# One attention-and-MLP kernel: the last attention unit's matrix work in another order

## The chip, the core and the metric

The kernel runs on one core of one Trainium2 chip. The metric is the device time of one execution in microseconds (us); the number given for a kernel is the median of several runs. A profiled execution is a separate run, recorded by the hardware profiler, with a span (first to last instruction) of its own.

## What is computed

A transformer block on 2048 rows of width 576: a layer norm whose scale and shift come from a condition vector, attention over the last 512 cached keys with 32 query heads and 16 key/value heads of width 128, a gated residual, a second such layer norm, a ReGLU MLP of width 4608, and a second gated residual. All of it is float32. Cut to what matters:

```python
h = _layernorm(x) * (1 + ca) + sa
q = (h @ wq)                                  # 32 heads of 128
scores = einsum("bhqd,bhkd->bhqk", q, k) * (Dh ** -0.5)
p = softmax(scores)                           # 512 keys
x = x + ga * (einsum("bhqk,bhkd->bhqd", p, v) @ wo)
h = _layernorm(x) * (1 + cb) + sb
x = x + gb * ((relu(h @ W_gate) * (h @ W_up)) @ W_down)
```

## The kernel before

A float32 operand is split into a high part (`hi`, rounded to the format the TensorE multiplies) and a low part (`lo`, the rest), and a product is made of three matmuls: high by high, high by low and low by high.

**Units.** The attention runs as 128 units (`NU = 128`), one for each pair of a query block of 512 rows and a head; units 0 to 127 are worked in a loop, and work of neighbouring units overlaps. For unit u the loop issues: the scores (`s_half`, 12 matmuls, L496 to L498, into two PSUM tiles `s`) with a transposing maximum on VectorE (L501); `max_pre` (L515, L516) and `sum_pre` of the unit before (L522); `spread` (L530, one small matmul `qm` that carries the maxima of this unit and the sums of the unit before across partitions); `max_bc`, which turns the maxima into a row to subtract; `exp_half` twice; `hi_half` and `lo_half`, which split the exponentials p (ScalarE L577, GpSimd L600); and the sums `ks` (VectorE L606, GpSimd L609). The product with the values (`pv`) of unit u-1 runs during unit u, then `o_mul` (VectorE L641), `o_hi` (ScalarE L645) and `o_lo` (GpSimd L649) make the split output of that unit.

**Output pieces.** Two heads together are multiplied with `wo` in pieces of 128 rows (`piece`, 12 matmuls at L660 into the PSUM tile `wo`, of which there is one buffer, `psW`). A piece takes `ohi` and `olo` of an even and an odd unit. Its result goes to `acc` either on VectorE (L671) or, for a seeded piece, as a copy on ScalarE (L669), which is put into the list `pend_act` and issued at the next `flush(pend_act)`.

**The last unit.** Unit 127 is one of those in which the subtraction of the maximum is done on TensorE (`by_pe`): ScalarE casts the row of maxima (`mr`, L569), and four matmuls with the matrix `minus` (L587) add it, negated, to the scores in PSUM; the exponential (L589) then reads PSUM. The tiles `s` of `psS` have two buffers. The MLP's first pair of products takes one of them: `new_banks` allocates the tile `gu` of the pair from the same pool and tag.

**The MLP.** `mlp_slots` is a generator; each `next` issues one of seven products of a block (two halves of 7 matmuls each at L1004, into `gu`), with pieces of other work between the halves. The steps `M0`, `M1`, `M2` issue the first three products; the first three remaining output pieces of units 124 and 125 (`filler`: `wo_1`, `wo_2`, `wo_3`) stand between their halves.

**What sets the order.** TensorE, VectorE, ScalarE and GpSimd run the instructions in the order in which the program issues them. Beside the loop there is a list of steps with times (`step(name, t, fn)`, unit u at time 10u; `e` is 1280); `run(u, k)` issues all steps up to time 10u+k. Steps of one time go in the order in which they were put down. The order of the DMA queue of SyncE is set by the framework. The three lines around which the rest turns are in the loop:

```python
        else:
            piece(at[10 * u + 1])
            pv_part(u - 1, False)
```

Of the kernel before, what the change touches and what calls it, by code (L numbers as in the profile page):

```python
# [34 lines left out]
def kernel(  # L35
# [120 lines left out]
    def gate_row(j):  # L156
        r = cp.tile([P, D], F32, tag="mrow", name=f"mrow{j}")
        mod_row(j, r, 0.0)
        return r
# [103 lines left out]
    pend, pend_act = [], []  # L263
# [3 lines left out]
    def flush(q=None):  # L267
        q = pend if q is None else q
        while q:
            q.pop()()  # L270
# [178 lines left out]
    NU = HKV * NQB * 2  # L449
# [10 lines left out]
    def unit(u):  # L460
        return UNITS[u]
# [3 lines left out]
    def qproj(u, lo, hi):  # L465
        g, qb, h = unit(u)
        if lo == 0:
            assert ready[qb] == "a"
            ps = psM.tile([P, 512], F32, tag="mm", name=f"qps{u}")
            qst[u] = ps, proj_ops(ps, wqs[h], hT[qb], u in (4, 6))  # L470
        for f in qst[u][1][lo:hi]:
            f()
# [12 lines left out]
    def by_pe(u):  # L485
        return u < PE0 or u >= NU - PE1
# [18 lines left out]
    def by_moves(u):  # L505
        return PE0 <= u < MOVES
# [39 lines left out]
    def sum_inv(u):  # L546
        nc.vector.reciprocal(t5[u + 1][:, 1, :], t5[u + 1][:, 1, :] if by_moves(u + 1) else bps[u + 1][:, 64:80])
# [7 lines left out]
    def max_bc(u):  # L555
        r = bps[u][:, 256:272] if by_pe(u) else t5[u][:, 0, :]
        if not by_moves(u):
            nc.vector.tensor_reduce(r, bps[u][:, :64].rearrange("p (a b) -> p b a", a=4), axis=AX.X, op=ALU.max)
            if u:
                sum_inv(u - 1)  # L560
        m = bp.tile([P, 512], F32, tag="bc", name=f"mb{u}")
        if by_pe(u):
            rr = sp.tile([P, 16, 2], F32R, tag="rr", name=f"rr{u}", bufs=1)
            nc.vector.tensor_copy(rr[:, :, 0], r)
            nc.vector.tensor_sub(rr[:, :, 1], r, rr[:, :, 0].bitcast(F32))
            nc.vector.transpose(m.rearrange("p (b s t) -> p b s t", s=2, t=16),
                                rr.bitcast(F32)[:, :, :, None].to_broadcast([P, 16, 2, 16]))
            bc[u] = bp.tile([P, 512], F32R, tag="bc", name=f"mr{u}")
            nc.scalar.copy(bc[u], m)  # L569
        else:  # L570
            nc.vector.transpose(m.rearrange("p (b j) -> p b j", j=32),
                                r[:, :, None].to_broadcast([P, 16, 32]))
            bc[u] = m
# [24 lines left out]
    def lo_half(u, h):  # L598
        lo_[u, h] = pp.tile([P, 2, 512], F32R, tag="lo", name=f"lo{u}_{h}", bufs=2)
        nc.gpsimd.tensor_sub(lo_[u, h], pt[u, h], hi_[u, h].bitcast(F32))  # L600
# [7 lines left out]
            for j in range(2):  # L608
                nc.gpsimd.tensor_tensor(ks_[u], ks_[u], p[:, j, :], op=ALU.add)  # L609

    def pv_part(u, lows):
        g, qb, hd = unit(u)
        if not lows:
            pvps[u] = psM.tile([P, 512], F32, tag="mm", name=f"pv{u}")
        ps, v = pvps[u], vs[g]
        for kt in range(4):
            a, b = (x[u, kt // 2][:, kt % 2, :] for x in (hi_, lo_))
            if lows:
                nc.tensor.matmul(ps, v[:, kt, :], b, start=False, stop=kt == 3)
            else:  # L620
                nc.tensor.matmul(ps, v[:, kt, :], a, start=kt == 0, stop=False)
                nc.tensor.matmul(ps, v[:, 4 + kt, :], a, start=False, stop=False)
        if lows:
            done[u] = pvps.pop(u)
# [18 lines left out]
    def o_hi(u):  # L643
        ohi[u] = op.tile([P, 512], F32R, tag="ohi", name=f"ohi{u}")
        nc.scalar.copy(ohi[u], o[u])  # L645

    def o_lo(u):
        olo[u] = op.tile([P, 512], F32R, tag="olo", name=f"olo{u}")
        nc.gpsimd.tensor_sub(olo[u], o.pop(u), ohi[u].bitcast(F32))  # L649
# [33 lines left out]
    w_use, pieces, seeds = set(), [], {}  # L683
# [590 lines left out]
    def step(name, t, fn, *args):  # L1274
        sched.append((t + PLAN.get(name, 0), len(sched), fn, args))

    HOOK = (0, 4, 6, 9)
    e = 10 * NU
# [11 lines left out]
    def setd(d, k, fn):  # L1290
        def go():
            d[k] = fn()
        return go
# [144 lines left out]
    step("m5.l", 1046, m5_back)  # L1438
    step("gb", 1059, setd(mods, "gb", lambda: gate_row(5)))

    step("T.ohi2", e, o_hi, NU - 2)
    step("T.olo2", e, o_lo, NU - 2)
    lay0, lay = lay_steps()
# [104 lines left out]
    mlp = mlp_slots()  # L1548
# [54 lines left out]
    mat(0, 1, lambda: h_back(0, "B22"))  # L1603
    for n, t in enumerate((1245, 1265, 1275)):
        step("w0", t, w_prep, n)
    step("M0", e, next, mlp)
    step("M1", e + 1, next, mlp)
    step("T.pv0", e + 2, pv_half, NU - 1, 0)
    step("T.pv1", e + 2, pv_half, NU - 1, 1)
# [10 lines left out]
    def run(u, k):  # L1620
        t = 10 * u + k
        while sched and sched[-1][0] <= t:
            fn, args = sched.pop()[2:]
            fn(*args)

    for u in range(NU):
        u0, q0 = (u - 4, 3) if u % 2 else (u - 3, 1)
        u1, q1 = (u - 2, 0) if u % 2 else (u - 3, 2)
        if u0 > 0:
            pieces.append((10 * u + (3 if u + 1 < NU else 1), u0, q0))  # L1630
        if u1 > 0:
            pieces.append((10 * u + 6, u1, q1))
    at = {t: n for n, (t, _, _) in enumerate(pieces)}

    run(-1, 9)
    for u in range(NU):
        run(u, 0)
        if u > 1 and u % 2 == 0:
            o_hi(u - 2)
            o_lo(u - 2)  # L1640
        s_half(u, 0)
        s_half(u, 1)
        run(u, .5)
        max_pre(u)
        if u:
            sum_pre(u - 1)
        if by_moves(u):
            cross(u)
            max_bc(u)
        run(u, 1)  # L1650
        if u + 1 < NU:
            qproj(u + 1, 0, 14)
        else:
            piece(at[10 * u + 1])
            pv_part(u - 1, False)
        run(u, 2)
        if not by_moves(u):
            spread(u)
            max_bc(u)
        if u + 1 < NU:  # L1660
            q_hi(u + 1)
        run(u, 3)
        if 10 * u + 3 in at:
            piece(at[10 * u + 3])
        if u > 1 and u % 2:
            o_hi(u - 2)
            o_lo(u - 2)
        run(u, 4)
        if u + 1 == NU:
            pv_part(u - 1, True)  # L1670
        elif u:
            pv_half(u - 1, 0)
        flush(pend_act)
        exp_half(u, 0)
        flush()
        run(u, 5)
        exp_half(u, 1)
        if late_hi(u):
            hi_half(u, 0)
        if u:  # L1680
            if by_moves(u):
                sum_inv(u - 1)
            sum_bc(u - 1)
        if u + 1 < NU:
            q_lo(u + 1)
        ksum_op(u, 0)
        ksum_op(u, 1)
        run(u, 6)
        if 0 < u < NU - 1:
            pv_half(u - 1, 1)  # L1690
        if 10 * u + 6 in at:
            piece(at[10 * u + 6])
        run(u, 7)
        if u:
            o_mul(u - 1)
        flush()
        run(u, 8)
        hi_half(u, 1)
        flush(pend_act)
        lo_half(u, 0)  # L1700
        lo_half(u, 1)
        run(u, 9)
# [56 lines left out]
```

## Time and profile before

| | |
|---|---|
| median of 3 runs | 2860.71 us (2859.68 to 2861.39) |
| the profiled execution's own time | 2863.24 us |
| its span | 2861.5 us |
| mean granted TensorE clock in it | 0.997 |
| attention units, about | 45 to 1606 us of the span |
| the stretch that the change reorders | 1583 to 1614 us |
| MLP, about | 1592 to 2861 us |

In the profile PE is TensorE's matmuls, PEld its weight loads, DVE is VectorE, ACT ScalarE, POOL GpSimd, SPq the DMA queue of SyncE. A timeline row gives the start in us from the span's start, the busy time, the engine, line and operation, output and inputs by name, and the count; in brackets stands the idle time before it and what ended it. A matmul's busy time is pipelined (0.39 us for one of 512 columns, of which the next starts 0.23 us later), so that stalls are read best from the starts of the weight loads, one to each matmul.

### The profile page before, as it was taken

How to read it: one execution, taken by the hardware profiler on the slowest of the kernel's cores; microseconds unless marked ns; L12 is line 12 of the kernel's file. 1: busy time of each engine (PE TensorE's matmuls, PEld its weight loads, DVE VectorE, ACT ScalarE, POOL GpSimd, SP SyncE). 2: the span in 40 equal slices, each digit the busy share in tenths (PEclk: the TensorE clock that was granted, in tenths of full speed). 3: DMA queues.
4: the chain of work that ended last, by engine and by line, in shares of the span. 5: the costliest groups of instructions: out<-in, count | busy, mean ns of one | idle time of the engine just before them, and what ended most of it. 6: DMA issues, size and time to landing. Idle time of an engine off the chain costs nothing.

```text
span 2861.5 us, 41171 instructions
## 1 busy us (share of the span) xinstructions
PE 2815.0 (98%) x15006; PEld 2449.6 (86%) x15006; DVE 2247.7 (79%) x3383; ACT 1476.5 (52%) x2105; POOL 2123.3 (74%) x1564
## 2 busy tenths in 40 slices
PE   6999999999999999999999999999999999999999
PEld 5788888888888888888888888888888888888888
DVE  7899999999888998888889756666676466666666
ACT  5666666666766666666656444444444122222221
POOL 5688888888899989877778666777777356655653
PEclk9999999999999999999999999999999999999999
DMA  4012132223233223312244456666667854444443
GB/s 162 24 45 79 65 106 85 83 81 101 96 104 94 92 63 128 106 69 86 72 150 139 157 209 219 233 237 230 234 234 262 337 165 154 153 155 162 155 154 106
DMA packets 164362, 399.57 MB, mean 140 GB/s; under 512 B 15040, under 2 KB 61888, under 8 KB 164160
## 3 DMA queue, kind: packets, MB, share of 16 engines
q1 hardware_dynamic: 132912, 284.84, 30.5%
q10 hardware_dynamic: 31248, 112.11, 9.9%
q8 instruction: 118, 1.93, 0.3%
q14 instruction: 84, 0.69, 0.1%
HBM read 271.16 MB, written 154.57 MB: 149 GB/s over the span
## 4 chain that ended last, share of the span: by engine, by line
PE 82%; POOL 6%; DVE 6%; ACT 2%; issue 2%; DMA 2%; SPq 0%; ACTq 0%; POOLq 0%; DVEq 0%
PE gu L1004 26%; PE wo L660 11%; PE qps L424 11%; PE md L660 8%; PE st_P L1106 6%; PE s L498 3%; PE s L496 3%; PE s L497 3%; PE pv L635 3%; PE pv L634 3%; PE pv L633 3%; POOL lo L600 2%; ACT p L593 1%; DVE t L501 1%; POOL wop L783 1%
## 5 line engine op out<-in xcount | busy, mean ns | idle before, releaser
L600 POOL TENSOR_TENSOR lo<-p,hi 128x1024 fp32r<-128x1024 f32 x256 | 610.4, 2405 | 1.1 <-ACT hi L577 1.1
L609 POOL TENSOR_TENSOR ks<-ks,p 128x512 f32<-128x512 f32 x256 | 351.4, 1373 | 240.3 <-DVE ks L606 133.3
L501 DVE TRANSPOSE_TENSOR_REDUCE t<-s 128x32 f32<-128x1024 f32 x256 | 313.8, 1239 | 85.1 <-PE s L498 75.7
L1004 PE MATMUL gu<-hop_B,wop 128*128 128x512 f32 x1512 | 374.9, 391 | 0.3 <-POOL wop L783 0.2
L1004 PEld LDWEIGHTS gu<-hop_B,wop 128*128 128x128 f32 x1512 | 275.1, 188 | 51.1 <-POOL wop L783 0.9
L1004 PE MATMUL gu<-hop_T,wop 128*128 128x512 f32 x1260 | 316.1, 391 | 0.0
L424 PE MATMUL qps<-hTa,wA 128*128 128x512 f32 x1288 | 309.8, 390 | 5.8 <-DVE hTa L372 2.3
L660 PE MATMUL wo<-woga,ohi 128*128 128x288 f32 x1472 | 298.7, 295 | 1.7 <-POOL woga L183 1.5
L591 DVE TENSOR_TENSOR p<-s,mb 128x1024 f32<-128x1024 f32 x246 | 290.3, 1219 | 4.2
L424 PEld LDWEIGHTS qps<-hTa,wA 128*128 128x128 f32 x1288 | 241.2, 188 | 59.2 <-DVE hTa L372 4.6
L476 ACT ACTIVATE qhi<-qps 128x512 fp32r<-128x512 f32 x128 | 76.4, 597 | 367.2 <-PE qps L424 359.3
L660 PE MATMUL md<-wogb,hhi 128*128 128x288 f32 x1280 | 260.1, 296 | 3.5 <-DVE acc L671 2.6
L660 PEld LDWEIGHTS wo<-woga,ohi 128*128 128x128 f32 x1472 | 246.1, 188 | 18.1 <-POOL woga L183 3.4
L1004 PEld LDWEIGHTS gu<-hop_T,wop 128*128 128x128 f32 x1260 | 227.8, 188 | 38.9
L577 ACT CAST hi<-p 128x1024 fp32r<-128x1024 f32 x256 | 259.5, 1042 | 1.5
L593 ACT ACTIVATE p<-p 128x1024 f32<-128x1024 f32 x246 | 249.5, 1052 | 13.8 <-DVE p L591 13.4
L671 DVE TENSOR_TENSOR acc<-md,acc 128x576 f32<-128x576 f32 x160 | 120.8, 755 | 165.0 <-PE md L660 164.6
L660 PEld LDWEIGHTS md<-wogb,hhi 128*128 128x128 f32 x1280 | 213.1, 189 | 16.5 <-DVE acc L671 4.2
L1115 DVE TENSOR_TENSOR acc<-st_P,acc 128x576 f32<-128x576 f32 x160 | 121.0, 756 | 127.9 <-PE st_P L1106 127.9
L660 PE MATMUL wo<-woga,olo 128*128 128x288 f32 x736 | 217.8, 296 | 1.3 <-POOL olo L649 1.2
L660 PE MATMUL md<-wogb,hlo 128*128 128x288 f32 x640 | 189.2, 296 | 0.0
L649 POOL TENSOR_TENSOR olo<-rb,ohi 128x512 fp32r<-128x512 f32 x128 | 167.2, 1307 | 15.3 <-ACT ohi L645 15.1
(278 smaller groups left out, 7094.4 us busy)
## 6 DMA issues: line engine op xcount, KB each, us to landing
wop<-wk_P SPq DMA_DIRECT2D x133, 640.0 KB
wk_P<-wop ACTq DMA_DIRECT2D x119, 640.0 KB
wr<-wlay SPq DMA_DIRECT2D x68, 384.0 KB
rogb<-wd SPq DMA_DIRECT2D x68, 288.0 KB
againq<-akq SPq DMA_DIRECT2D x18, 640.0 KB
rwA<-wq SPq DMA_DIRECT2D x32, 320.0 KB
wlay<-wg SPq DMA_DIRECT2D x36, 256.0 KB
roga<-wo SPq DMA_DIRECT2D x32, 288.0 KB
```

The lines of the kernel that those rows point to most:

```text
L424: return [lambda i=i, a=a, b=b: nc.tensor.matmul(ps, a, b, start=(i == 0), stop=(i == n - 1)) for i, (a, b) in enumerate(ops)]
L501: nc.vector.tensor_reduce(t5[u][:, 2 * h:2 * h + 2, :].rearrange("p k b -> p (k b)"), t.rearrange("p k (b j) -> p (k b) j", j=32), axis=AX ...
L577: nc.scalar.copy(hi_[u, h], pt[u, h])
L591: nc.vector.tensor_tensor(p, t, bc[u][:, None, :].to_broadcast([P, 2, 512]), op=ALU.subtract)
L593: nc.scalar.activation(p, p, AF.Exp, bias=0.0, scale=1.0)
L600: nc.gpsimd.tensor_sub(lo_[u, h], pt[u, h], hi_[u, h].bitcast(F32))
L609: nc.gpsimd.tensor_tensor(ks_[u], ks_[u], p[:, j, :], op=ALU.add)
L649: nc.gpsimd.tensor_sub(olo[u], o.pop(u), ohi[u].bitcast(F32))
L660: nc.tensor.matmul(ps[:, half, :H2], a[:, sl], w[b][:, cs], start=(n == 0 and seed is None), stop=(n == 5), skip_group_check=seed is not None)
L1004: nc.tensor.matmul(ps, a, c, start=s not in heir(m) and i == 0 and s not in seeds_of(m), stop=i == len(ops) - 1, skip_group_check=True)
L1106: nc.tensor.matmul(ps[:, j, :H2], x[:, sl], w[:, y, :], start=n == 0 and not second, stop=n == 2, skip_group_check=True)
L1115: nc.vector.tensor_tensor(t, ps[:, :, :H2], t, op=ALU.add)
```

## The change

For unit 127 alone, and for the products of unit 126 that fall into it:

- the product of unit 126 with the values is cut: its high parts for the first two key tiles (4 matmuls, L621 and L622) come first, then the small matmul `qm` of unit 127, then the high parts for the other two key tiles (4 matmuls);
- the output piece `wo_0` of units 124 and 125 (12 matmuls) moves from behind the subtraction (L587) to in front of it;
- the low parts of unit 126 (4 matmuls, L619), its `o_mul`, `o_hi` and `o_lo` move behind the MLP's first product, `M0`;
- `M0` comes one step earlier, so that it stands ahead of those low parts;
- `o_hi` and `o_lo` of unit 125 move from unit 127 to the end of unit 126, in front of the two `lo_half` of unit 126;
- `flush(pend_act)` is called right after the first four matmuls of the product, so that the copy of the seeded piece `wo_3` to `acc` (ScalarE L669) comes in front of the cast of the maxima.

No instruction is added or removed.

```diff
-    def pv_part(u, lows):
+    def pv_part(u, lows, kts=range(4)):
         g, qb, hd = unit(u)
-        if not lows:
+        if not lows and not kts[0]:
             pvps[u] = psM.tile([P, 512], F32, tag="mm", name=f"pv{u}")
         ps, v = pvps[u], vs[g]
-        for kt in range(4):
+        for kt in kts:
...
+    step("T.low", e, pv_part, NU - 2, True)
+    step("T.mul", e, o_mul, NU - 2)
     step("T.ohi2", e, o_hi, NU - 2)
     step("T.olo2", e, o_lo, NU - 2)
...
-    step("M0", e, next, mlp)
+    step("M0", e - 1, next, mlp)
...
-            pieces.append((10 * u + 6, u1, q1))
+            pieces.append((10 * u + (6 if u + 1 < NU else 3), u1, q1))
...
             piece(at[10 * u + 1])
-            pv_part(u - 1, False)
+            pv_part(u - 1, False, range(2))
+            flush(pend_act)
         run(u, 2)
...
+        if u + 1 == NU:
+            pv_part(u - 1, False, range(2, 4))
...
-        if u > 1 and u % 2:
+        if u > 1 and u % 2 and u + 1 < NU:
             o_hi(u - 2)
             o_lo(u - 2)
         run(u, 4)
-        if u + 1 == NU:
-            pv_part(u - 1, True)
-        elif u:
+        if 0 < u < NU - 1:
             pv_half(u - 1, 0)
...
-        if u:
+        if 0 < u < NU - 1:
             o_mul(u - 1)
...
         flush(pend_act)
+        if u + 2 == NU:
+            o_hi(u - 1)
+            o_lo(u - 1)
         lo_half(u, 0)
         lo_half(u, 1)
```

TensorE in unit 127, before, from the last high parts of unit 126 (`pv`) through `qm`, the low parts and the subtraction (`s<-mr,minus`) to the piece `wo_0` (the `againo` are weights):

```order
L621 MATMUL pv_16631<-hi_1_16589,againv_16210 128x512
L622 MATMUL pv_16631<-hi_1_16589,againv_16210 128x512
L530 MATMUL qm_16615<-t_127_16605,quad 128x80
L619 MATMUL pv_16631<-lo_0_16594,againv_16210 128x512 x2
L619 MATMUL pv_16631<-lo_1_16596,againv_16210 128x512 x2
L587 MATMUL s_0_16598<-mr_16648,minus 128x512 x2
L587 MATMUL s_1_16607<-mr_16648,minus 128x512 x2
L660 MATMUL wo_0_16677<-againo_16174,ohi_16471 128x288 x2
```

With the change, TensorE at the same place, from the high parts of the second key tile on:

```order
L622 MATMUL pv_16635<-hi_0_16543,againv_16210 128x512
L530 MATMUL qm_16619<-t_127_16609,quad 128x80
L621 MATMUL pv_16635<-hi_1_16589,againv_16210 128x512
L622 MATMUL pv_16635<-hi_1_16589,againv_16210 128x512
L621 MATMUL pv_16635<-hi_1_16589,againv_16210 128x512
L622 MATMUL pv_16635<-hi_1_16589,againv_16210 128x512
L660 MATMUL wo_0_16655<-againo_16174,ohi_16471 128x288 x2
```

and, after the rest of `wo_0`, the subtraction with what follows it, the MLP's first product:

```order
L660 MATMUL wo_0_16655<-againo_16176,olo_16596 128x288
L587 MATMUL s_0_16602<-mr_16649,minus 128x512 x2
L587 MATMUL s_1_16611<-mr_16649,minus 128x512 x2
L1004 MATMUL gu_16693<-hop_B_0_16355,wop_16291 128x512 x2
L1004 MATMUL gu_16693<-hop_B_3_16358,wop_16291 128x512
```

So `qm` has moved in front of four of the high parts, `wo_0` in front of the subtraction, and the first product now follows the subtraction at once; the four low parts come later, between `wo_2` and the second product.

ScalarE in the same stretch, before (`mr` is the cast of the maxima, `p` the exponential, `q` the copy of the first product):

```order
L693 COPY wo_3_16592<-acc_132 128x2x288
L569 CAST mr_16648<-mb_16643 128x512
L645 CAST ohi_16650<-rb_16550 128x512
L669 COPY acc_132<-wo_3_16592 128x576
L589 ACTIVATE p_0_16659<-s_0_16598 128x1024
```

and with the change:

```order
L693 COPY wo_3_16592<-acc_132 128x2x288
L645 CAST ohi_16594<-rb_16550 128x512
L669 COPY acc_132<-wo_3_16592 128x576
L569 CAST mr_16649<-mb_16644 128x512
L589 ACTIVATE p_0_16668<-s_0_16602 128x1024
```

The output cast of unit 125 and the copy of `wo_3` have moved from behind the cast of the maxima to in front of it. Farther down the queue the cast of unit 126's output has moved from in front of the copy `q` to behind it.

On GpSimd the low part of unit 125's output (L649) has moved in front of the two low parts of unit 126's exponentials (L600). On VectorE the addition of `wo_0` to `acc` (L671) moves from behind the sum `ks` (L606) and `o_mul` of unit 126 to in front of the transposes of `rb` (L552), and `o_mul` of unit 126 goes behind the additions of `wo_1` and `wo_2`. On SyncE's queue one load of an MLP weight (`wop`, the sixth) moves in front of two loads `wr`.

## The prediction

> **What bounds the kernel now.** I read the page first.
>
> ```profile
> span 2861.5 us, 41171 instructions
> ...
> PE 2815.0 (98%) x15006; PEld 2449.6 (86%) x15006; DVE 2247.7 (79%) x3383; ACT 1476.5 (52%) x2105; POOL 2123.3 (74%) x1564
> ...
> PE 82%; POOL 6%; DVE 6%; ACT 2%; issue 2%; DMA 2%; SPq 0%; ACTq 0%; POOLq 0%; DVEq 0%
> ```
>
> TensorE is busy 98% of the span and carries 82% of the chain that ended last, so only time in which it stands can be won. The change touches some thirty of 2861 us; what it can win is what TensorE loses there. That is read from the chain of waits in order of time, around unit 127:
>
> ```profile
> 1584.50 4.01 POOL lo L600 x2
> 1588.56 0.74 PE pv L619 x2
> ...
> 1590.33 1.91 PE wo L660 x12
> 1592.24 1.61 PE gu L1004 x7
> ...
> 1597.04 1.58 PE wo L660 x12
> ```
>
> The chain leaves TensorE once: the low parts of unit 126 wait for GpSimd. A clean group of 7 matmuls of 512 columns takes 1.61 us (0.23 each), a clean output piece 1.58; the piece behind the subtraction took 1.91. How long TensorE stood is seen in the timeline, from the starts of the weight loads:
>
> ```profile
> 1585.39 0.19 PEld L621 LDWEIGHTS pv<-hi,againv 128*128 128x128 f32 x1
> ...
> 1586.31 0.42 PEld L530 LDWEIGHTS qm<-t,quad 128*128 128x128 f32 x2
> ...
> 1588.55 0.30 PEld L619 LDWEIGHTS pv<-lo,againv 128*128 128x128 f32 x2 [1.59 <-POOL lo L600]
> ...
> 1589.14 0.76 PEld L587 LDWEIGHTS s<-mr,minus 128*128 128x128 f32 x4 [0.29 <-ACT mr L569]
> ...
> 1590.20 0.30 PEld L660 LDWEIGHTS wo<-againo,ohi 128*128 128x128 f32 x2 [0.30 <-ACT acc L669]
> ...
> 1591.94 1.48 PEld L1004 LDWEIGHTS gu<-hop_B,wop 128*128 128x128 f32 x7
> ...
> 1598.33 0.32 PEld L1004 LDWEIGHTS gu<-hy_T,wop 128*128 128x128 f32 x2
> ```
>
> The orders part at 1585.39, ahead of the last four high parts, and meet at the second product, 1598.33: 12.94 us. Work in it: 12 matmuls of 512 columns (4 high, 4 low, 4 of the subtraction) at 0.23, 2.76; `qm`, 0.22 to the next load (below); three pieces, 4.74; two products, 3.22. Sum 10.94. So TensorE loses 2.00 us here, 0.07% of the time: the most that this stretch can give.
>
> **The change part by part.** No instruction comes or goes, so each term is a wait.
>
> *`qm` in front of four high parts.* It needs the sums of unit 126, which VectorE finishes last. The same step of unit 126, where TensorE had nothing else, shows the delays.
>
> ```profile
> 1573.37 0.70 DVE L522 TRANSPOSE_TENSOR_REDUCE t<-ks 128x16 f32<-128x512 f32 x1
> ...
> 1574.13 0.30 PEld L530 LDWEIGHTS qm<-t,quad 128*128 128x128 f32 x2 [0.30 <-DVE t L522]
> ...
> 1574.35 0.30 PEld L660 LDWEIGHTS wo<-againo,ohi 128*128 128x128 f32 x2
> ...
> 1574.62 0.22 DVE L558 TENSOR_REDUCE t<-qm 128x16 f32<-128x64 f32 x1 [0.54 <-PE qm L530]
> ...
> 1585.44 0.71 DVE L522 TRANSPOSE_TENSOR_REDUCE t<-ks 128x16 f32<-128x512 f32 x1
> ...
> 1586.92 0.23 DVE L558 TENSOR_REDUCE qm<-qm 128x16 f32<-128x64 f32 x1 [0.78 <-PE qm L530]
> ...
> 1588.47 0.62 ACT L569 CAST mr<-mb 128x512 fp32r<-128x512 f32 x1 [5.52 <-DVE mb L566]
> ```
>
> L522 ends at 1586.15 in unit 127, and nothing ahead of it on VectorE moves. `qm` loads 0.06 later (1574.07 to 1574.13), at 1586.21. TensorE reaches it at 1585.39: it now stands 0.82 us where it stood not at all, since the four high parts were the cover. What is won is the maxima: L558 follows the load by 0.49 (1574.13 to 1574.62), so it starts at 1586.70 instead of 1586.92, and the cast `mr`, 1.55 behind it as before, at 1588.25. It ends at 1588.87, and the subtraction can load 0.05 later (1589.09 to 1589.14 before), at 1588.92.
>
> *`wo_0` in front of the subtraction.* From 1586.21 TensorE needs 0.22 for `qm`, 0.92 for four high parts and 1.58 for `wo_0`: 1588.93. So it comes to the subtraction as `mr` is done, and the waits for the low parts (1.59 on the loads), for `mr` (0.29) and for the copy of `wo_3` (0.30) are gone. `wo_0` needs the copy out of the only `psW` buffer and unit 125's split output:
>
> ```profile
> 1582.31 0.64 ACT L693 COPY wo<-acc 128x576 f32<-128x576 f32 x1
> ...
> 1583.78 4.72 POOL L600 TENSOR_TENSOR lo<-p,hi 128x1024 fp32r<-128x1024 f32 x2
> ...
> 1589.69 1.29 POOL L649 TENSOR_TENSOR olo<-rb,ohi 128x512 fp32r<-128x512 f32 x1 [1.19 <-ACT ohi L645]
> ```
>
> ScalarE is free from 1582.95; the cast `ohi`, even if it waits until `wo_3` has used the buffer it takes (near 1584.4), is done by 1585.0, the copy L669, as large as L693's 0.64, follows `wo_3`'s end (just before the high parts, near 1584.9), by 1585.7; `olo` then runs on GpSimd from about 1585.1 to 1586.4. `wo_0` starts at 1587.35. The two `lo` come behind it and end at about 1591.1 instead of 1588.50, with SyncE's next load `wr` behind them; their matmuls now stand at 1597, and that load's first reader (L811, whose first row is at 1621.9) is far off. All this I cost at nothing.
>
> *The first product right behind the subtraction.* It takes a PSUM buffer of the tiles `s`, and these have two: the first half's, free once its exponential has read it. Before, `wo_0` and 1.74 us lay between; now nothing does. The first units show the same reuse, and what it costs:
>
> ```profile
> 47.87 1.02 ACT L589 ACTIVATE p<-s 128x1024 f32<-128x1024 f32 x1 [0.82 <-PE s L587]
> ...
> 48.95 0.29 PEld L496 LDWEIGHTS s<-qhi,kv 128*128 128x128 f32 x1 [1.04 <-ACT p L589]
> ...
> 70.45 0.80 PEld L587 LDWEIGHTS s<-mr,minus 128*128 128x128 f32 x4
> ...
> 71.25 1.03 ACT L589 ACTIVATE p<-s 128x1024 f32<-128x1024 f32 x1 [0.36 <-PE s L587]
> ...
> 1590.05 1.03 ACT L589 ACTIVATE p<-s 128x1024 f32<-128x1024 f32 x1
> ...
> 1592.06 1.02 ACT L589 ACTIVATE p<-s 128x1024 f32<-128x1024 f32 x1
> ```
>
> The exponential starts 0.80 behind the subtraction's first load, takes 1.02, and the next load comes 0.06 after it: 1588.93 + 1.88 = 1590.81. TensorE is through with the subtraction at 1589.85, so it stands 0.96 us. The cover was `wo_0`, which has gone elsewhere.
>
> *The low parts behind the first product.* The first product starts at 1590.81, 1.13 earlier than before, but four low parts (0.92) that were then done are still owed. They wait for nothing at 1597. The second product starts at 1598.33 - 1.13 + 0.92 = 1598.12. **Sum: 0.21 us earlier**; stalls of 0.82 + 0.96 = 1.78 in place of 2.00.
>
> *What is late next.* Behind `M0`, unit 126's `o_mul` waits for the low parts (1598.2 instead of 1591.72), its cast on ScalarE ends near 1599.7, and the casts `hy_T` queued behind it start there.
>
> ```profile
> 1598.05 1.14 ACT L881 CAST hy_T<-lfb 128x512 fp32r<-128x512 f32 x2
> ...
> 1602.22 5.50 POOL L894 TENSOR_TENSOR hz_T<-lfb,hy_T 128x512 fp32r<-128x512 f32 x4
> ...
> 1612.36 0.41 PEld L1004 LDWEIGHTS gu<-hy_T,wop 128*128 128x128 f32 x2
> ...
> 1613.23 1.29 POOL L649 TENSOR_TENSOR olo<-rb,ohi 128x512 fp32r<-128x512 f32 x1 [0.37 <-ACT ohi L645]
> ...
> 1614.69 0.19 PEld L660 LDWEIGHTS wo<-againo,olo 128*128 128x128 f32 x1
> ```
>
> They are 1.6 late, but GpSimd reads them only from 1602.22, and TensorE wants the result at 1612.36. Tight is only the last unit's `olo`: done at 1614.52, loaded at 1614.69. Its chain starts at TensorE's own products and moves with them. I cost both at nothing.
>
> Bounds: if both new stalls were absent, a gain of 2.00; if the product had to wait for the second exponential (1592.06 in place of 1590.05 for the first, so 2.0 more), a loss of 1.8. The value taken lies between, by the rows of units 0 to 2, which show these very waits.
>
> The profiled execution took 2863.24 us, of which 2861.5 are span, and is 2.5 above the median shown; 0.21 less makes 2863.0 there, and 2860.5 for the median.
>
> **Rivals.** *The first product gets the other buffer.* Then it waits for the second exponential: 2.0 later, 0.21 - 2.0 = 1.8 slower than before, 2862.5. It decides if that buffer is the one the pool hands out. For it: nothing in the profile names the buffer. Against: before, the first product loaded at 1591.94, while the second exponential ran from 1592.06. Chance 0.08. TensorE would stand 3 us in one piece, and another row tells what that can cost:
>
> ```profile
> 1914.13 0.85 PE L660 MATMUL md<-wogb,hhi 128*128 128x288 f32 x2 [2.40 <-DVE acc L671]
> ...
> 1914.13 3.23 PE md L660 x12
> ...
> 1900.00:1960.00 60.00, 57.60 (x307) 50.69 (x306) 40.13 (x35) 23.46 (x33) 44.86 (x39) 0.97 0.60 220
> ...
> L811 DVE TENSOR_TENSOR wr<-wr,wr x17: 945/947/6071, 1621.9 to 2195.9; 128x768 f32<-128x768 f32 x17
> ```
>
> After a stall of 2.40 us the next 12 matmuls took 3.23 instead of 1.58 (half speed; the granted clock of that stretch is 0.97): 1.65 more. With that this rival ends at 2864.1. The Trainium skill ("TensorE: Matmul & The Clock Gate", Part 1) has the clock halve after an idle window of about 3.4 us; by it the rival stays at 2862.5. The row at 1914 shows a shorter stall do it, so the measurement decides; the stalls I forecast, 0.82 and 0.96, are under both, and 1.59 here before cost no clock (the product behind it ran in 1.61).
>
> *No stall at the product or at `qm`.* The gain is 2.00, 2858.7. Against: L522's end and the reuse at 48.95. Chance 0.10.
>
> *The MLP falls out differently.* One subtraction of VectorE (L811), right before that stall of 2.40, took 6.07 us instead of 0.95, and the addition behind it (L671) came late; the slow clock added 1.65. A shift of some tenths may undo this, or make another. That is 4.05 either way: 2856.4, or 2864.5. For it: the same operation took between 0.945 and 6.071. Against: nearly all that runs there is released by TensorE and moves with it. Chance 0.11 each. The Trainium skill ("SBUF — State Buffer", "SBUF: two separate sides") says that such an operation and GpSimd hold a shared port pair for a whole instruction; by it the wait would be at most one GpSimd instruction, some 1.3 us by the row of `olo`, and this stall would not be there; the row of 6.07 against 0.95 is longer, so the trace does not agree.
>
> **How the numbers follow.** The forecast, 2860.5, with its own range 2859.7 to 2861.4 (the runs before spread by 1.7), has 0.60; the rivals 0.08, 0.10, 0.11 and 0.11. The range takes in both ends of the MLP's case and all between: 2856.4 to 2864.5. About 0.2% (5.7 us) is what a measurement of this kernel can tell from no change; no case reaches it alone, two together would: faster 0.03, within 0.2% 0.93, slower 0.04.
>
> **What would show it.** In the changed profile: `qm`'s load waits 0.8 us on L522; the subtraction waits for nothing or a tenth; the first `gu` load waits about 1 us on the exponential L589; the low parts wait for nothing; the second product comes 12.7 us after the fifth high part's place instead of 12.9. I am wrong if the first product starts without a wait or only after the second exponential, or if the MLP shows one stall of 2 us more or less.

## The result, and the profile after

| | before | changed |
|---|---|---|
| median, first comparison (22 runs each) | 2861.03 us (2856.68 to 2868.05) | 2865.05 us (2861.85 to 2869.15) |
| mean | 2860.87 | 2865.47 |
| ratio of the times | | 1.0017, 95% interval 1.0011 to 1.0023 |
| profiled execution, span | 2861.5 | 2866.8 |
| granted TensorE clock | 0.997 | 0.997 |

The change makes the kernel 0.17% slower, some 4.6 us by the means. The page of the changed kernel answers to the lines shown of before:

```profile
span 2866.8 us, 41171 instructions
...
PE 2816.5 (98%) x15006; PEld 2450.9 (85%) x15006; DVE 2247.8 (78%) x3383; ACT 1476.6 (52%) x2105; POOL 2124.6 (74%) x1564
...
PE 82%; DVE 6%; POOL 5%; ACT 2%; issue 2%; DMA 2%; SPq 0%; ACTq 0%; POOLq 0%; DVEq 0%
```

The counts and the busy times are those of the same work; what grew is waiting, and the page doesn't tell where. So I fix four points of the program in each trace (starts of weight loads): the first score load of unit 127, the second product's first load, the first load of unit 127's own first output piece, and the first `md` load, from which on all is MLP.

| us from the first score load of unit 127 | before | changed |
|---|---|---|
| that load itself, from the span's start | 1580.23 | 1580.90 |
| second product | 18.10 | 17.81 |
| unit 127's first output piece | 33.71 | 33.69 |
| first `md` load | 51.25 | 52.66 |
| from there to the end of the span | 1230.0 | 1233.2 |

The 5.3 us between the two spans are thus 0.7 ahead of the reordered stretch, 1.4 in it, and 3.2 in the MLP, where no instruction moved on TensorE. Up to the second product the change did what was forecast. The timeline of the changed kernel's weight loads:

```profile
1586.87 0.30 PEld L530 LDWEIGHTS qm<-t,quad 128*128 128x128 f32 x2 [0.84 <-DVE t L522]
...
1589.59 0.79 PEld L587 LDWEIGHTS s<-mr,minus 128*128 128x128 f32 x4
...
1591.52 1.46 PEld L1004 LDWEIGHTS gu<-hop_B,wop 128*128 128x128 f32 x7 [1.14 <-ACT p L589]
...
1597.89 0.78 PEld L619 LDWEIGHTS pv<-lo,againv 128*128 128x128 f32 x4
1598.71 0.42 PEld L1004 LDWEIGHTS gu<-hy_T,wop 128*128 128x128 f32 x2
...
1613.11 0.30 PEld L1004 LDWEIGHTS gu<-hy_T,wop 128*128 128x128 f32 x2 [0.33 <-issue]
...
1615.44 0.30 PEld L660 LDWEIGHTS wo<-againo,ohi 128*128 128x128 f32 x2 [0.31 <-ACT ohi L645]
1616.79 0.19 PEld L660 LDWEIGHTS wo<-againo,olo 128*128 128x128 f32 x1 [1.05 <-POOL olo L649]
```

The two new stalls are there, the subtraction waits for nothing, and the second product is 0.29 us earlier. The last three rows are new: TensorE waits 0.33 us for something that the profile doesn't name, 0.31 for ScalarE's `ohi` and 1.05 for GpSimd's last `olo`. That is 1.69, all of what the way from the second product to the first `md` load has grown by (33.15 to 34.85). GpSimd's timeline tells why the last and longest wait is there. Before:

```profile
1595.78 4.77 POOL L600 TENSOR_TENSOR lo<-p,hi 128x1024 fp32r<-128x1024 f32 x2
1600.51 1.74 POOL L649 TENSOR_TENSOR olo<-rb,ohi 128x512 fp32r<-128x512 f32 x1
```

and changed:

```profile
1598.72 4.78 POOL L600 TENSOR_TENSOR lo<-p,hi 128x1024 fp32r<-128x1024 f32 x2 [2.49 <-PE pv L619]
1603.44 1.77 POOL L649 TENSOR_TENSOR olo<-rb,ohi 128x512 fp32r<-128x512 f32 x1
1605.16 5.94 POOL L894 TENSOR_TENSOR hz_T<-lfb,hy_T 128x512 fp32r<-128x512 f32 x4
...
1615.47 1.27 POOL L649 TENSOR_TENSOR olo<-rb,ohi 128x512 fp32r<-128x512 f32 x1 [0.34 <-ACT ohi L645]
```

GpSimd's first `lo` of unit 127 now stands 2.49 us until the low parts of unit 126 (L619) have been multiplied. Those products, moved to 1597.89, read the two `lo` tiles of unit 126, and there are only two such tiles (`bufs=2`): the next `lo` can't be written before. Counted from the first score load, this `lo` starts 17.82 us on where it was 15.55, and all that follows on GpSimd is late, down to the last `olo`: 34.57 where it was 33.00.

In the MLP two TensorE stalls of the changed profile weren't in before's, and one of before's is gone:

| VectorE or DMA event, us behind the first `md` load | before | changed |
|---|---|---|
| 276: an operation L811 `wr<-wr,wr` that adds or subtracts two weight tiles (a "sum" below), and TensorE's wait behind it | 6.07, waits 2.83 | 0.95, none |
| 347: the same sum two blocks on | 0.95, none | 6.07, waits 2.83 |
| 605 to 608: the load of a weight `wop` at the MLP's half change (where the second of its two halves begins) | waits 0.30 | waits 3.54 |

### The profile page after: what moved, and what is told of

Its sections match the earlier page's. It is cut to its first block, busy times and chain, and to the rows that moved or that the text cites. A ratio compares the mean times of both kernels' runs of the same rounds, so it can differ in the third digit from the quotient of the medians.

```text
span 2866.8 us, 41171 instructions
## 1 busy us (share of the span) xinstructions
PE 2816.5 (98%) x15006; PEld 2450.9 (85%) x15006; DVE 2247.8 (78%) x3383; ACT 1476.6 (52%) x2105; POOL 2124.6 (74%) x1564
## 4 chain that ended last, share of the span: by engine, by line
PE 82%; DVE 6%; POOL 5%; ACT 2%; issue 2%; DMA 2%; SPq 0%; ACTq 0%; POOLq 0%; DVEq 0%
PE gu L1004 26%; PE wo L660 11%; PE qps L424 11%; PE md L660 8%; PE st_P L1106 6%; PE s L498 3%; PE s L496 3%; PE s L497 3%; PE pv L635 3%; PE pv L634 3%; PE pv L633 3%; POOL lo L600 2%; DVE t L501 1%; DVE p L591 1%; POOL olo L649 1%
## 5 line engine op out<-in xcount | busy, mean ns | idle before, releaser
L600 POOL TENSOR_TENSOR lo<-p,hi 128x1024 fp32r<-128x1024 f32 x256 | 610.7, 2406 | 3.6 <-PE pv L619 2.5
L671 DVE TENSOR_TENSOR acc<-md,acc 128x576 f32<-128x576 f32 x160 | 120.8, 755 | 169.1 <-PE md L660 168.6
L649 POOL TENSOR_TENSOR olo<-rb,ohi 128x512 fp32r<-128x512 f32 x128 | 167.3, 1307 | 16.0 <-ACT ohi L645 15.8
```

## The experiments

Beside a median I give differences of means, with their standard error (from the spread of the 11 runs, and of the runs of before measured beside them).

**1. Both kernels once more: `again_before`, `again_after`.**

> The kernel before against itself. Ratio 1.000. The stretch from the scores of unit 127 to the first md: 51.25 us within 0.2. If the stall on the wop load near 2240 us belongs to the change, it is absent here; if it is chance, it may be here too.

> The changed kernel once more, unaltered. Stretch from the first score load of unit 127 to the first load of an MLP piece (md): 51.25 us before, 52.66 in the changed kernel's profile. Both theories of that stretch expect 52.7 again within 0.2. The rest of the difference of the two spans, 3.2 us, came from one stall of TensorE near 2241 us, where a load of an MLP weight (wop) took 9.9 us to land. If the change causes that stall, it is there again, and the time is 4 us above before; if it is chance of the transfers, it is there in some profiles only, of either kernel, and the time is nearer 2 us above before.

Before: 2860.28 us, ratio 0.9999 (0.999 to 1.0008). Changed: 2865.35, ratio 1.0013 (1.0004 to 1.0022), by the means 4.5 ± 0.7 us. The stretch repeats to hundredths (51.26 and 52.68 to the first `md` load). The MLP doesn't: the second profile of the changed kernel has the long sum in both places, at 276 and at 347, and no wait at the half change (0.54). So 1.4 us of the loss are fixed in place, and some 3 come with events that move about.

**2. Own buffers for the first `lo` of unit 127: `ownbuf`.** The changed kernel, in which this `lo` goes into two free tiles of another pool, so that it need not wait for L619:

```diff
+        if (u, h) == (NU - 1, 0):
+            lo_[u, h] = [xp.tile([P, 640], F32R, tag="xm", name=f"lx{j}")[:, :512] for j in range(2)]
+            for j in range(2):
+                nc.gpsimd.tensor_sub(lo_[u, h][j], pt[u, h][:, j, :], hi_[u, h].bitcast(F32)[:, j, :])
+            return
...
```

> The changed kernel, but the first low part of unit 127's exponentials is written to two tiles of another pool (xm), so that it needs no buffer of unit 126's low parts. Theory 1 (the two buffers of lo: GpSimd waits 2.5 us at 1596 until the moved low-part matmuls have read them, and all behind it on GpSimd is late): that wait is gone, olo of unit 127 comes in time, the stretch is about 51.0 us, 1.7 less than the changed kernel, and the time about 1.7 less. Theory 2 (the casts hy_T stand behind unit 126's output cast on ScalarE and VectorE's chain to the last output is late for that alone; GpSimd's wait costs nothing): the stretch stays at 52.7.

GpSimd's timeline, this version:

```profile
1593.64 2.55 POOL L602 TENSOR_TENSOR lx<-p,hi 128x512 fp32r<-128x512 f32 x2
1596.26 2.40 POOL L605 TENSOR_TENSOR lo<-p,hi 128x1024 fp32r<-128x1024 f32 x1
1598.62 1.29 POOL L655 TENSOR_TENSOR olo<-rb,ohi 128x512 fp32r<-128x512 f32 x1
```

The wait is gone (and with it all three of TensorE's), `olo` of unit 126 comes 2.3 us sooner (20.22 us from the first score load instead of 22.54), and the first `md` load stands at 51.01: 1.65 better than the change and 0.24 better than before. ScalarE's casts, the rival's cause, stand where the change put them. So the two `lo` buffers carry the local loss. The time, 2862.86 us (ratio 1.0009, 1.0 to 1.0018; means 2.1 ± 0.9 over before), is still not better than before.

**3. Low parts between the subtraction and the first product: `lowbetween`.** There they cover TensorE's wait for the exponential, and GpSimd gets its buffers early:

```diff
-    step("T.low", e, pv_part, NU - 2, True)
-    step("T.mul", e, o_mul, NU - 2)
-    step("T.ohi2", e, o_hi, NU - 2)
+    step("T.low", e - 1, pv_part, NU - 2, True)
+    step("T.mul", e - 1, o_mul, NU - 2)
+    step("T.ohi2", e - 1, o_hi, NU - 2)
...
-            o_lo(u - 1)
         lo_half(u, 0)
+        if u + 2 == NU:
+            o_lo(u - 1)
         lo_half(u, 1)
```

> The changed kernel, but the four low-part matmuls of unit 126, its o_mul and its output cast stand between the subtraction and the first product, and on GpSimd olo of unit 125 goes between the two low parts. Both theories expect the late olo to be gone. Beyond that the low parts (0.92 us) now fill the wait of the first product for the exponential (1.14 us on its load in the changed kernel), so the second product comes 0.9 us earlier against the scores than in the changed kernel (16.9 us after the scores, 17.81 there, 18.10 before), and the stretch to the first md is 50.1 us: 1.1 below before, 2.6 below the changed kernel. Time 1 us below before, if the MLP goes as before.

The stretch is as expected, 50.11 (1.14 better than before), and the wait at the first product is down from 1.14 to 0.22. The time is not: 2861.70 us, ratio 1.0003 (0.9994 to 1.0012), means 1.1 ± 0.8 over before. Again 2 us are lost in the MLP. Its profile has the long sum at 347 and a wait of 3.29 at the half change.

**4. Parts alone: `lowonly`, `lowfirst`.** The first is the kernel before with only the low parts (and their multiplication) moved behind the first product; the second is the change with only these put back in front of it (first and second diff).

```diff
+    step("T.low", e, pv_part, NU - 2, True)
+    step("T.mul", e, o_mul, NU - 2)
-    step("M0", e, next, mlp)
+    step("M0", e - 1, next, mlp)
...
```

```diff
-    step("T.low", e, pv_part, NU - 2, True)
+    step("T.low", e - 1, pv_part, NU - 2, True)
```

> The kernel before with one part of the change alone: the low parts of unit 126 and their multiplication moved behind the MLP's first product, the orders of qm, of the subtraction and of wo as before. If the two lo buffers carry the local loss: GpSimd's first lo of unit 127 waits 2 to 2.5 us for these products, the last olo (before at +33.0 from the first score load of unit 127) comes 2 us later, and the first md load stands at +52.5 to +52.9 instead of +51.25; the time is 1.3 us up with this and up to 4.6 with what the MLP adds: 2862 to 2865.4. If the loss came from the other two parts (qm amid the high parts, wo in front of the subtraction): first md load at +51.3 and 2861.

> The changed kernel with the low parts of unit 126 and their multiplication back in front of the MLP's first product, behind the subtraction; olo of unit 126 behind both lo on GpSimd as in the change. If the two lo buffers carry the local loss: the first lo of unit 127 waits for nothing, the last olo comes at +32 to +33 from the first score load of unit 127 (changed kernel +34.6), the first md load at +50.1 to +51.0 instead of +52.66, and the time 1.5 to 2.5 us under the changed kernel: 2863 to 2864. If the loss came from the other two parts: first md load still at +52 to +52.7.

In `lowonly` a row of the weight loads and one of GpSimd read:

```profile
1587.18 0.76 PEld L587 LDWEIGHTS s<-mr,minus 128*128 128x128 f32 x4 [2.40 <-ACT mr L569]
```

```profile
1598.53 4.76 POOL L600 TENSOR_TENSOR lo<-p,hi 128x1024 fp32r<-128x1024 f32 x2 [4.68 <-PE pv L619]
```

`lowonly` took 2864.01 us (ratio 1.001, 1.0001 to 1.0019; means 2.5 ± 0.7 over before). The wait for the `lo` buffers is there with nothing else of the change, and from the second product to the first `md` load it takes 34.87 us (before 33.15, changed 34.85): 1.7 us, the same price. But the first `md` load came at 55.12, not at 52.5 to 52.9. My expectation had forgotten that the low parts were TensorE's cover for the maxima: without them, and with `qm` and `wo_0` in their old places, the subtraction waits 2.40 us for the cast `mr`, and a slow clock follows (below). In `lowfirst` GpSimd's `lo` waits for nothing. The first `md` load comes at 51.45, a little over the 50.1 to 51.0 expected, and a row of TensorE's loads shows what holds it:

```profile
1614.03 0.19 PEld L660 LDWEIGHTS wo<-againo,olo 128*128 128x128 f32 x1 [0.54 <-POOL olo L649]
```

TensorE is 0.39 us earlier at this piece than before, GpSimd's last `olo` 0.3 later, and the slack was 0.17. (The low parts themselves now wait 0.95 for unit 126's `lo`, which the change has put behind `olo` of unit 125; the wait of the first product for the exponential goes into that.) The time is 2862.57 us, by the means 2.2 ± 0.8 under the 33 earlier runs of the changed kernel. The low parts behind the product are the wrong step; `lowbetween` has all the other parts of the change (with `olo` of unit 125 one place later), and its stretch is better than before.

**5. The sums in the MLP: `before_s3first`, `after_s3first`, `lowbetween_s3first`.** In all blocks of the MLP the sum L811 `wr<-wr,wr` is put in front of the evacuation of the product P5 (VectorE's L1200 and L1201) instead of behind it:

```diff
-        for k, s in {1: [(0, "S1")], 2: [(0, "S4")], 5: [(1, "S3")], 6: [(1, "S2")]}.get(i, []):
+        for k, s in {1: [(0, "S1")], 2: [(0, "S4")], 4.5: [(1, "S3")], 6: [(1, "S2")]}.get(i, []):
...
+                if i == 4:
+                    sums(m, 4.5)
                 if not early:
                     (evac_seeded if 0 < m < NFP else evac)(m, s)
```

> The kernel before with one edit, in the MLP alone: VectorE's sum L811 wr<-wr,wr of the next block is put in front of the evacuation of P5 (L1200, L1201) instead of behind it, in every block. In five of the six profiles so far this sum takes 6.07 us in one or two blocks (276 and 347 us behind the first md product), each time when it starts 0.07 to 0.55 us after GpSimd has begun its chain L782, L783, L183, L1144; where it starts 0.2 to 0.5 us before GpSimd it takes 0.95. Theory A (what of the change's loss the lo buffers do not explain is this race, which each kernel enters with another offset): at the new place the sum starts 2.8 us earlier, while GpSimd is at L855 or idle, takes under 2 us, the TensorE waits of 2.83 us at +282 and +354 go with their half clock of 3.4 us, and the time is 2860.8 - 4.5 = 2856.3, from 2854 to 2858. Theory B (the loss is in other places, and the race is hidden or replaced): 2859 to 2862.

> The same edit in the changed kernel. Theory A: both races gone, and the distance to the kernel before with the same edit falls from 4.6 us to the local loss of 1.4 us by the lo buffers (up to 3 where the wop load at the half change waits): 2857.7 to 2859.5. Theory B: the distance stays 4 to 5 us whatever the level, so 2860 to 2865.

> The same edit in the version with the low parts between the subtraction and the MLP's first product. Theory A: its gain of 1.15 us up to the first md product is now seen in the time: about 1 us under the kernel before with the same edit, 2855 to 2857, and so 4 us under the kernel before. Theory B: 1 us over the kernel before with the same edit, as without it.

The why of the edit is read from VectorE's and GpSimd's timelines at 347. Before:

```profile
1981.57 0.95 DVE L811 TENSOR_TENSOR wr<-wr,wr 128x768 f32<-128x768 f32 x1
```

```profile
1981.78 1.33 POOL L782 TENSOR_TENSOR wop<-wr,wop 32x256 fp32r<-32x256 f32 x1 [1.83 <-ACT wop L781]
```

Changed:

```profile
1980.16 6.07 DVE L811 TENSOR_TENSOR wr<-wr,wr 128x768 f32<-128x768 f32 x1
1986.15 0.74 DVE L671 TENSOR_TENSOR acc<-md,acc 128x576 f32<-128x576 f32 x1
```

```profile
1980.09 0.75 POOL L782 TENSOR_TENSOR wop<-wr,wop 32x256 fp32r<-32x256 f32 x1 [1.83 <-ACT wop L781]
1980.80 1.29 POOL L783 TENSOR_TENSOR wop<-wr,wop 128x512 fp32r<-128x512 f32 x1
1982.06 1.43 POOL L183 TENSOR_TENSOR wogb<-rogb,wogb 128x576 fp32r<-128x576 f32 x1
1983.45 1.28 POOL L1144 TENSOR_TENSOR hlo<-c,hhi 128x512 fp32r<-128x512 f32 x1
1984.70 0.71 POOL L782 TENSOR_TENSOR wop<-wr,wop 32x256 fp32r<-32x256 f32 x1
1985.38 1.98 POOL L783 TENSOR_TENSOR wop<-wr,wop 128x512 fp32r<-128x512 f32 x1
```

Before, the sum starts 0.21 us ahead of GpSimd's L782 and takes 0.95. Changed, it starts 0.07 behind it and ends only in GpSimd's sixth instruction; the addition L671, and TensorE with it, wait for the sum. Which of the two engines starts first is the race that the theories speak of.

Both theories missed the level: 2866.92, 2868.64 and 2865.66 us (before beside them 2861.64; ratios 1.0019, 1.0025 and 1.0013). The long sums did go (at both places 0.95 to 2.1 us), but the early sum delays others, and in three other blocks of the kernels before and changed it takes some 4 us itself (at 167, 383 and 419 behind the first `md` load; in `lowbetween` at 167 and 418 alone). Groups of TensorE's weight loads in the first half of the MLP (busy us and mean ns, then us idle ahead of them and what ended most of it), this edit in the kernel before:

```profile
L660 PEld LDWEIGHTS md<-wogb,hhi 128*128 128x128 f32 x1011 | 167.3, 188 | 16.6 <-DVE acc L671 8.0
...
L1004 PEld LDWEIGHTS gu<-hy_T,wop 128*128 128x128 f32 x475 | 86.4, 188 | 19.5 <-POOL wop L783 4.5
```

and the kernel before without it:

```profile
L660 PEld LDWEIGHTS md<-wogb,hhi 128*128 128x128 f32 x1014 | 169.3, 189 | 12.5 <-DVE acc L671 3.3
...
L1004 PEld LDWEIGHTS gu<-hy_T,wop 128*128 128x128 f32 x480 | 87.1, 188 | 16.3 <-POOL wop L783 1.1
```

4.7 us more on L671, though the one long stall has gone from it, and 3.4 more on L783, in many small waits. What the three do tell is the distance between kernels once the sum is out of those two places, which was theory A's other claim: changed minus before fell from 4.6 to 1.0 ± 0.6 us, `lowbetween` minus before from +1.1 to -1.0 ± 0.6. That agrees with the stretch alone (1.4 and -1.1), but `lowbetween` has one sum of 4 us fewer than the other two, so the second figure isn't clean.

**6. The same in two blocks only: `before_s3two`, `after_s3two`, `lowbetween_s3two`.** The edit of 5 with `m in (8, 10)`, the blocks at 276 and 347.

> The kernel before with the sum L811 wr<-wr,wr in front of the evacuation of P5 in two blocks alone (m = 8 and 10), where it took 6.07 us (276 and 347 us behind the first md product); in all blocks the same edit took the two long sums away and lost 4 us by short waits in the other blocks. Theory A (a race of VectorE with GpSimd in these two blocks makes the residual): neither sum is over 4 us, no TensorE wait of 2.83 us, last load at +1222 to +1223 us behind the first md product instead of +1225.4, time 2857 to 2858.5. Theory B (other places): +1225 and 2860 to 2862.

> The same two blocks in the changed kernel. Theory A: last load at +1222 to +1223 (+1226 where the wop load of the half change waits 3 us), and 1.4 us (the lo buffers) to 2.5 us over the kernel before with the same edit: 2858.5 to 2860.5. Theory B: 4 to 5 us over it, 2864 to 2866.

> The same two blocks in the version with the low parts between the subtraction and the MLP's first product. Theory A: about 1 us under the kernel before with the same edit: 2856 to 2857.5, that is 3.5 to 5 us under the kernel before. Theory B: 1 us over the kernel before.

Measured, beside a before of 2860.07 (mean 2860.94 ± 0.49): 2860.07, 2862.45 and 2859.51 us (means 2860.02 ± 0.33, 2862.57 ± 0.56, 2859.13 ± 0.34). The longest of these sums is now 2.4 us:

```profile
L811 DVE TENSOR_TENSOR wr<-wr,wr x17: 942/946/2367, 1619.2 to 2190.0; 128x768 f32<-128x768 f32 x17
```

(of `before_s3two`: shortest, median and longest in ns; changed kernel 944/947/6073). The distances: changed minus before 2.55 ± 0.65, `lowbetween` minus before -0.9 ± 0.5, where 1.4 to 2.5 and -1 were expected, against 4.6 and +1.1 without the edit. Both sets together: 1.8 ± 0.45 and -0.95 ± 0.4. The levels lie some 2 us over theory A's. The kernel before, from which the edit took a long sum, gained only 0.9 ± 0.6 by the means and nothing by the medians, where theory A had 2 to 4; its time is theory B's. From the first `md` load to the last load it took 1223.74, 1222.51 and 1222.87 us, as forecast or 0.7 over; in the kernel before the stall at the half change, 1.79, came instead:

```profile
2232.09 3.02 PEld L1004 LDWEIGHTS gu<-hop_B,wop 128*128 128x128 f32 x14 [1.79 <-issue]
```

Nor did the edit end the meeting with GpSimd. The part L1201 of the evacuation now stands where the sum stood, and in `before_s3two` it reads:

```profile
1905.40 3.74 DVE L1201 SCALAR_TENSOR_TENSOR c<-c 128x512 f32<-128x512 f32 x1
```

In the kernel before it takes 0.69 there. In all three versions, at both places, it takes 3.74 to 3.76. So the edit made this outcome alike in all three, which is what the distances need, but it didn't make the places free of cost (TensorE still stands 1.16 us at 281 in `before_s3two`, at most 0.8 there in the other two).

`lowbetween_s3two` has the lowest time of all versions: 1.8 ± 0.6 us under before by the means, 0.6 by the medians. The interval of its ratio, 0.9988 to 1.0006, doesn't exclude that nothing was gained.

**All profiles side by side.** Where the sum L811 starts against GpSimd's L782 (behind it is +), its duration, and the wait at the half change:

| | 1st `md` load | to last load | at 276 | at 347 | half change |
|---|---|---|---|---|---|
| before | 51.25 | 1225.44 | +0.55: 6.07 | -0.21: 0.95 | 0.30 |
| again_before | 51.26 | 1225.83 | +0.45: 6.05 | -0.21: 0.95 | 0.49 |
| lowonly | 55.12 | 1222.47 | -2.05: 0.95 | -0.21: 0.95 | 0.47 |
| changed | 52.66 | 1228.73 | -0.50: 0.95 | +0.07: 6.07 | 3.54 |
| again_after | 52.68 | 1227.73 | +0.31: 6.07 | +0.06: 6.07 | 0.54 |
| ownbuf | 51.01 | 1223.95 | -2.05: 0.95 | +0.08: 6.07 | 0.54 |
| lowbetween | 50.11 | 1227.90 | -2.06: 0.94 | +0.09: 6.08 | 3.29 |
| lowfirst | 51.45 | 1223.83 | -2.06: 0.94 | +0.09: 6.07 | 0.40 |

`lowonly` has none of the three events and is the floor: against it the `md` additions L671, counted from the first `md` load, fall behind at each long sum, by 2.0 to 2.1 us in the three cases in which the clock stays and by 3.4 to 3.7 in the five in which it halves (below), and by up to 3.2 at the half change. At 347 the sum is long in all five profiles of the four kernels that have `qm` and `wo_0` moved and short in all three of the two kernels that haven't, and the offset is fixed to 0.03 us. That is an agreement in eight profiles; no run moved this offset alone. SyncE's queue isn't what sets it: `lowbetween` and `lowfirst` have its order of before, `lowonly` that of the change, `ownbuf` one of its own. A difference between the two sorts of kernel is there early. ScalarE's copy L1178, the row before and the row changed:

```profile
1668.47 1.00 ACT L1178 COPY gu<-gu 128x1024 f32<-128x1024 f32 x1 [5.25 <-PE gu L1004]
```

```profile
1670.26 1.00 ACT L1178 COPY gu<-gu 128x1024 f32<-128x1024 f32 x1 [4.95 <-PE gu L1004]
```

That is 36.99 and 36.70 us behind the first `md` load, in the same three and five profiles. From there VectorE runs 0.13 to 0.15 us ahead of before, and 0.04 to 0.11 by 267; how that becomes the 0.28 by which the offsets at 347 differ was not followed. At 276 the landing of a DMA decides. GpSimd's step ahead of its chain, before and changed:

```profile
1898.73 1.29 POOL L845 TENSOR_TENSOR hx_T<-hx_T 128x512 f32<-128x512 f32 x1 [1.14 <-DMA hx_T<-hb]
```

```profile
1901.99 1.62 POOL L845 TENSOR_TENSOR hx_T<-hx_T 128x512 f32<-128x512 f32 x1 [2.37 <-DMA hx_T<-hb]
```

This step starts 267.25 us behind the first `md` load in the one and 268.43 in the other (266.48 in `lowbetween`), and GpSimd's L782 comes earlier or later accordingly. The VectorE instruction that starts next behind L782 is the long one. Where L782 starts at 274.56 to 275.16 (the four rows with -2.05 or -2.06), that is L1201, with 3.3 to 3.8 us instead of 0.7, and TensorE stands 0.3 to 0.8 us. At 275.31 to 275.51 it is the sum. At 276.31 (`changed`) the sum is already running, and neither is long.

**Left open.** Why the copy L1178 is released 0.29 us sooner, since both rows name the same product, and whether the offset at 347 comes from it. What moves the landing ahead of 276 (the sum was long there in 2 of 2 profiles of before and in 1 of 5 with the change). What decides whether a stall costs the clock. And the half change: over 1 us in `changed`, `lowbetween`, `before_s3two` and `lowbetween_s3two`, under 0.6 in all others, with no relation to how late TensorE came; nothing was tried against it.

## Why the prediction was wrong

The forecast was 2860.5, 0.21 us earlier than before, within 2856.4 to 2864.5; measured were 2865.05 and 2865.35. The stalls below are the idle times in the rows; counted from start to start, as the forecast did, the first two new ones are 0.79 and 1.01.

- *`qm` in front of four high parts*: a new stall of 0.82 forecast, 0.84 measured.
- *`wo_0` in front of the subtraction*: all waits there gone, as forecast.
- *First product behind the subtraction*: 0.96 forecast, 1.14 measured, on the first exponential; the rival of the other buffer fell. The second product came 0.29 us earlier (0.21 forecast).
- *The low parts behind the first product*: this step failed. "They wait for nothing" is true, but I asked only what they wait for, not who waits for them. I did note that the `lo` "matmuls now stand at 1597", looked for readers of SyncE's load behind them, and wrote "All this I cost at nothing". The writer that needs their tiles is GpSimd's next `lo`, which had followed `ks` without a wait at 1595.78. It now starts at 1598.72.
- *What is late next*: "I cost both at nothing" is the same failure one step on. "Tight is only the last unit's `olo`", 0.17 us of slack, was right; "its chain starts at TensorE's own products and moves with them" was not, since GpSimd's queue, 1.6 us late at this `olo`, is also in it. Price: 1.7 us from the second product to the first `md` load, shown by taking the wait away (`ownbuf`, 1.65; `lowfirst`, 1.2) and by making it alone (`lowonly`, 1.7).
- *The MLP falls out differently*: the mechanism of this rival was right, L811 at 6.07 in place of 0.95, and a stall of 2.4 (2.83 by the weight loads) behind it. Its size wasn't: 4.05 counted the slow clock as part of it, and the traces have 3.4 to 3.7 with it and 2.0 to 2.1 without. Nor were its chances. I took it as even, 0.11 each way, and looked at the one place that before had. Moved by some tenths, the same race is lost at a second place, and lost in every profile (347, 5 of 5), while the first isn't surely won. With the sum out of both places the distance between the kernels falls from 4.6 to 2.55 ± 0.65 (two blocks) or 1.0 ± 0.6 (all blocks). So the race is the likely cause of 2 us or more of the 3 that the stretch leaves unexplained; as the times of `before_s3two` didn't come down as they should, its exact share isn't shown. The stall at the half change may be the rest, and its link to the change isn't shown.

The Trainium skill ("SBUF — State Buffer", "SBUF: two separate sides") lets such an operation and GpSimd hold a shared port pair for one whole instruction. The prediction read this as a wait of at most the one instruction met, which the section doesn't say. Here the sum of 6.07 us sat through five GpSimd instructions in a row and ended in the sixth, which took 1.98 us instead of 1.29.

## What to carry to other kernels

When a reader is moved later, look at the tile it reads: how many buffers, and who writes the next one; with two buffers the price falls on the writer's engine, and on whatever that engine does last. When two engines' queues meet within some tenths of a microsecond at a far place, a small change ahead of it can decide that meeting anew: measure the moved stretch by itself between fixed points of the trace, and compare the kernels once more with the same outcome forced at the meeting places in both. Look there at what has come into the place of the instruction that was moved. A version whose gain is shown in the stretch (here 1.1 us) can still show none in the time.

## What the runs showed of the hardware

**A VectorE instruction behind GpSimd's chain.** VectorE's L811 takes 0.95 us if it starts 0.2 us or more ahead of GpSimd's L782, and 6.05 to 6.08 in all eight cases in which it starts 0.06 to 0.55 us behind it, with five GpSimd instructions following one another without a gap. L1201 takes 3.3 to 3.8 instead of 0.7 when it is the one behind L782.

**One and the same stall halves the clock or doesn't.** In `lowonly`, whose TensorE stood 2.40 us at 1587.18, the chain of waits reads

```profile
1587.19 1.28 PE s L587 x4
1588.46 3.03 PE wo L660 x12
1591.49 1.72 PE gu L1004 x7
```

with 3.03 us for an output piece that takes 1.58. The 12 matmuls behind the long sum of the changed profile took 2.71, by its chain of waits,

```profile
1986.95 2.71 PE md L660 x12
```

and the granted clock of the 7 us around them was 0.76 (busy us of PE, PEld, DVE, ACT and POOL, then clock, DMA share and GB/s):

```profile
1984.00:1991.00 7.00, 4.59 (x19) 3.89 (x18) 5.12 (x5) 1.45 (x2) 6.13 (x6) 0.76 0.78 294
```

Each of the eight long sums makes TensorE stand 2.40 us (2.83 by the weight loads), but the clock halves, to 0.50 for 3.4 us, behind five of them alone. `again_after` has both kinds, here the 6 us behind its first long sum and behind its second:

```profile
1913.00:1919.00 6.00, 5.88 (x31) 5.16 (x32) 4.36 (x7) 1.46 (x2) 3.75 (x4) 1.00 0.63 224
1986.00:1992.00 6.00, 6.00 (x25) 5.16 (x26) 3.07 (x5) 1.45 (x2) 3.52 (x4) 0.72 0.64 227
```

The longer stalls at the half change (3.54 by the loads in `changed`, 3.29 in `lowbetween`) cost no clock, and those of 0.84 and 1.14 us didn't either. So among stalls of 2.4 to 3.5 us, by the loads, the length alone doesn't decide it.

**The same kernel spreads by 10 us.** 33 runs of before beside the last experiment lie between 2857.85 and 2867.74, ten of them over 2862, while the stretch up to the MLP repeats to some hundredths. With the sum moved in two blocks, 11 runs of `before_s3two` lie between 2858.40 and 2861.98, but 11 of `after_s3two` between 2859.64 and 2866.29.
